# Warm-up matmuls from a constant, row tile 1 centred into its own buffer, final waits placed earlier: three small edits at the two ends of a TensorE-bound kernel

## The chip, the cores and the metric

The kernel runs on one core of a Trainium2 chip. The metric is the device time of one execution in microseconds (us). TensorE (PE in the profile) does the matmuls and PEld is its weight load; VectorE is DVE, ScalarE is ACT, GpSimd is POOL, SyncE is SP and issues all the DMA transfers. Every job also ran the kernel before on the same chip.

## The reference

```python
xn = layernorm(x)                       # x: 2048 x 512, bf16
y  = x + attention(xn) + geglu(xn)
# attention: 32 heads of 16, each query sees 8 keys at distance 0, 2, .. 14
# geglu: (gelu(xn @ w_gate) * (xn @ w_up)) @ w_down, inner size 1376
```

## The kernel before

The kernel is a graph of tasks. A list scheduler in the kernel's own code orders the tasks on each engine at build time, and another function turns dependencies into semaphore waits. So an edit at the start can change the order of matmuls far behind it.

The three places that the change touches. First, the warm-up: matmuls on a buffer of zeros that keep TensorE busy until data is there.

```python
G.task("dve", "c_wsrc", 0.25, lambda e: e.memset(wsrc[:, :], 0.0), wr=[I_wsrc], prio=PC - 1)
# ...
WARM = cfg.get("WARM", ([512] * 8 + [128], [512, 128]))   # before / behind the first transposes
for i, wn in enumerate(WARM[0] + WARM[1]):
    # ...
    e.matmul(PS[...], lhsT=wsrc[:, 0:128], rhs=wsrc[:, 0:wn], start=True, stop=True)
```

Second, row tile 1 (rows 128 to 255). Its statistics are taken on ScalarE, while VectorE does those of tile 0. ScalarE computes the sum, minus the mean, the sum of squares about the mean, the variance and the square root; VectorE subtracts the mean in place and multiplies by the reciprocal.

```python
("sxx1", 0.55, dict(out=XR[:, 0, :], func=ACTF.Square, bias=sums[:, 1:2],
                    accum_out=sums[:, 2:3]), ...),          # reads XIN row tile 1
("var1", 0.2, dict(out=mv[:, 1, 1:2], in_=sums[:, 2:3], func=ACTF.Identity, scale=1.0 / D), ...)
# ... sub1, on VectorE: in place, so it waits for sxx1
e.tensor_scalar(out=XIN[:, it.slot, t2, :], in0=XIN[:, it.slot, t2, :], scalar1=mv[:, t, 0:1],
                scalar2=None, op0=ALU.subtract)
```

ScalarE's order in the head is fixed by a chain: sum, square root 0, minus mean, squares, variance, square root 1, then the eviction of tile 0's transposes.

Third, the end. Before it ends, the kernel waits until all DMA semaphores have reached their totals. Those that don't belong to the last five DMAs are waited for just in front of the last store.

```python
if eng_name == "sp" and t is self.order["sp"][-1]:
    late = self.order["sp"][-5:]
    for (s, tot) in self.dma_totals:
        if not any(q.sem is s for q in late):
            e.wait_ge(s, tot)
```

## Time and profile before

| | before |
|---|---|
| time, median of 3 runs | 194.56 us (194.54 to 194.84) |
| span of the profiled run | 193.2 us (its own time 194.91) |
| TensorE busy | 187.6 us, 97% |
| first warm-up matmul | 1.51 us |
| first real QKV matmul | 6.23 us |
| TensorE goes on behind the second eviction | 7.95 us |
| last add ends, last store issued | 191.08, 191.26 us |

The time is a little longer than the span (194.91 against 193.20 us for the same execution). **t0** is the start of the first QKV matmul. **T** is the moment at which TensorE goes from half to full clock; it is read from the distance between starts of 128-column matmuls, 107 ns before and 56 ns after. Half and full clock are names for these two spacings: the profile's own clock column reads 1.00 on both sides of T. The **resume** is the first matmul behind ScalarE's second eviction (7.95 here): from there on TensorE is hardly ever without work. The prediction shows the lines.

### The profile page before, as it was taken

The page shows a single profiled execution, that of the slowest core. Times are in us where ns is not written, and L with a number is a line of the kernel's source. Part 1 is how long each engine was busy: PE and PEld are TensorE (multiplying, and loading weights), DVE is VectorE, ACT ScalarE, POOL GpSimd, SP SyncE. Part 2 cuts the span into 40 slices and gives each one's busy share as a digit, 9 for nine tenths or more (in the row PEclk, how much of TensorE's full clock was granted, in tenths as well). Part 3 has the DMA queues.
Part 4 walks back from the last instruction along what each step waited for, and adds up shares of the span by engine and source line. Part 5 has one row for each costly group of instructions (what it writes and reads, how often), then busy time and mean ns, then how long its engine had stood idle before and what let it go on. Part 6 is the DMA issues. An engine that isn't in the chain of part 4 may idle for free.

```text
span 193.2 us, 3285 instructions
## 1 busy us (share of the span) xinstructions
PE 187.6 (97%) x1239; PEld 92.6 (48%) x1256; DVE 152.4 (79%) x240; ACT 106.1 (55%) x177; POOL 15.7 (8%) x31
## 2 busy tenths in 40 slices
PE   6999999999999999999999999999999999999994
PEld 2794444444444444444444444444444444444484
DVE  5699999999997975999995599998996099912132
ACT  5677565786897666703376677328276720058000
POOL 6010011110931020000000000000000000000000
PEclk9999999999999999999999999999999999999999
DMA  5999997899564014975500597420250497130121
GB/s 142 352 397 327 313 171 136 215 244 226 150 128 102 3 33 132 242 144 150 151 25 27 127 243 166 117 90 0 68 132 21 112 230 163 41 112 0 48 76 44
DMA packets 34801, 27.04 MB, mean 140 GB/s; under 512 B 11265, under 2 KB 33249, under 8 KB 34785
## 3 DMA queue, kind: packets, MB, share of 16 engines
q1 hardware_dynamic: 34784, 26.83, 57.0%
q8 instruction: 10, 0.16, 0.4%
q14 instruction: 7, 0.05, 0.1%
HBM read 19.99 MB, written 5.26 MB: 131 GB/s over the span
## 4 chain that ended last, share of the span: by engine, by line
PE 97%; issue 1%; DVE 0%; DVEq 0%
PE PS L1399 36%; PE PS L1478 20%; PE PS L1156 18%; PE PS L1474 7%; PE PS L1102 4%; PE PS L1367 4%; PE PS L1240 4%; PE PS L870 2%; PE PS L1434 2%; PE PS L1233 1%; PE PS L1044 1%; DVE OB L1498 0%; DVE wsrc L819 0%; DVE Wd L843 0%; DVEq L558 0%
## 5 line engine op out<-in xcount | busy, mean ns | idle before, releaser
L1416 ACT ACTIVATE UU<-PS 128x512 bf16<-128x512 f32 x40 | 24.1, 603 | 35.7 <-PE PS L1399 35.7
L1478 PE MATMUL PS<-Wd,HT 128*128 128x512 bf16 (+2 forms) x207 | 41.1, 345 | 0.1
L1399 PE MATMUL PS<-xnT,Wu 128*128 128x512 bf16 x155 | 39.8, 379 | 0.7 <-issue 0.5
L1399 PE MATMUL PS<-xnT,Wg 128*128 128x512 bf16 x155 | 39.2, 379 | 0.5 <-ACT OT L1379 0.2
L1210 DVE TENSOR_TENSOR UNI<-QT,KT 128x2048 bf16<-128x2048 bf16 x32 | 37.0, 1219 | 2.6 <-PE PS L1367 2.5
L1156 PE MATMUL PS<-xnT,Wqkv 128*128 128x512 bf16 x156 | 35.3, 379 | 0.2
L1421 DVE TENSOR_TENSOR HT<-GG,UU 128x512 bf16<-128x512 bf16 x40 | 16.6, 419 | 20.2 <-ACT UU L1416 20.1
L1409 ACT ACTIVATE GG<-PS 128x512 bf16<-128x512 f32 x40 | 23.7, 601 | 15.0 <-PE PS L1399 12.2
L1478 PEld LDWEIGHTS PS<-Wd,HT 128*128 128x128 bf16 x209 | 19.6, 98 | 18.6
L1399 PEld LDWEIGHTS PS<-xnT,Wu 128*128 128x128 bf16 x160 | 15.3, 98 | 19.6 <-issue 1.3
L1399 PEld LDWEIGHTS PS<-xnT,Wg 128*128 128x128 bf16 x160 | 15.5, 98 | 19.3 <-ACT OT L1379 0.4
L1156 PEld LDWEIGHTS PS<-xnT,Wqkv 128*128 128x128 bf16 x160 | 15.6, 98 | 18.6
L1347 DVE TENSOR_TENSOR BS<-BS,PT 128x2048 bf16<-128x2048 bf16 x16 | 19.6, 1223 | 0.4
L1347 DVE TENSOR_TENSOR UNI<-BS,PT 128x2048 bf16<-128x2048 bf16 x16 | 19.5, 1218 | 0.0
L1498 DVE TENSOR_TENSOR OB<-PS,XR 128x512 bf16<-128x512 f32 (+2 forms) x19 | 11.2, 604 | 10.0 <-PE PS L1478 9.9
L1474 PE MATMUL PS<-Wo,OT 128*128 128x512 bf16 (+2 forms) x76 | 16.9, 345 | 0.0
L1180 ACT ACTIVATE VT<-PS 128x512 bf16<-128x512 f32 x16 | 9.6, 597 | 4.4 <-PE PS L1156 4.4
L1379 ACT ACTIVATE OT<-PS 128x512 bf16<-128x512 f32 x16 | 8.3, 602 | 5.0 <-PE PS L1367 5.0
L944 DVE BATCH_NORM_STATS2 st<-XIN 128x6 f32<-128x512 bf16 x15 | 10.1, 686 | 0.9 <-DMA XIN<-in_A_x_dram 0.9
L1474 PEld LDWEIGHTS PS<-Wo,OT 128*128 128x128 bf16 x76 | 7.2, 98 | 7.0
L1196 POOL COPY KT<-KT 128x64 bf16<-128x64 bf16 x3 | 8.0, 2657 | 17.5 <-ACT KT L1173 16.1
L1166 ACT ACTIVATE QT<-PS 128x512 bf16<-128x512 f32 x12 | 7.2, 597 | 3.1 <-PE PS L1156 3.1
(73 smaller groups left out, 153.6 us busy)
## 6 DMA issues: line engine op xcount, KB each, us to landing
BS<-vt_scratch SPq DMA_DIRECT2D x64, 128.5 KB, 3.7
vt_scratch<-VT SPq DMA_DIRECT2D x16, 128.0 KB
XR<-in_A_x_dram SPq DMA_DIRECT2D x16, 128.0 KB, 2.3
out_dram<-OB SPq DMA_DIRECT2D x14, 128.0 KB, 1.8
Wqkv<-in_A_wqkv_dram SPq DMA_DIRECT2D x3, 512.0 KB
XIN<-in_A_x_dram SPq DMA_DIRECT2D x6, 256.0 KB, 4.5
Wg<-in_B_w_gate_dram SPq DMA_DIRECT2D x1, 1280.0 KB
Wu<-in_B_w_up_dram SPq DMA_DIRECT2D x1, 1280.0 KB
```

Source lines behind the costliest of these rows:

```text
L944: return lambda e: e.bn_stats(out=st[:, t, :], in_=XIN[:, it.slot, t2, :])
L1156: ins = e.matmul(PS[:, 512 * it.slot:512 * it.slot + HWD], lhsT=lhsT, rhs=xnT[:, itx.slot, kt, c0:c0 + HWD], start=(kt == 0), stop=(kt == 3))
L1180: return lambda e: e.activation(out=VT[:, ito.slot, 0:HWD], in_=PS[:, 512 * it.slot:512 * it.slot + HWD], func=ACTF.Identity)
L1210: return lambda e: e.tensor_tensor(out=UNI[:, it.slot, :, :], in0=bass.AP(QT, (itq.slot * 4 + g) * 512, [[NQT * 4 * 512, 128], [0, 4], [1, ...
L1347: return lambda e: e.tensor_tensor(out=dst(), in0=bass.AP(BS, it.slot * 4 * 514 + o, [[NBS * 4 * 514, 128], [514, 4], [128, 4], [1, 128]]) ...
L1399: ins = e.matmul(PS[0:M, 512 * it.slot:512 * it.slot + 512], lhsT=Wx[:, kt, j * 128:j * 128 + M], rhs=xnT[:, itx.slot, kt, :], start=(kt = ...
L1409: return lambda e: e.activation(out=GG[0:M, ito.slot, :], in_=PS[0:M, 512 * it.slot:512 * it.slot + 512], func=ACTF.Gelu_apprx_tanh)
L1416: return lambda e: e.activation(out=UU[0:M, ito.slot, :], in_=PS[0:M, 512 * it.slot:512 * it.slot + 512], func=ACTF.Identity)
L1421: return lambda e: e.tensor_tensor(out=HT[0:M, ito.slot, j, :], in0=GG[0:M, ig.slot, :], in1=UU[0:M, iu.slot, :], op=ALU.mult)
L1474: ins = e.matmul(PS[:, 512 * it.slot:512 * it.slot + CW], lhsT=OT[:, ito.slot, dq, ti * 128:(ti + 1) * 128], rhs=Wo[:, dq, c0:c1], start=( ...
L1478: ins = e.matmul(PS[:, 512 * it.slot:512 * it.slot + CW], lhsT=HT[:, ith.slot, j, ti * 128:(ti + 1) * 128], rhs=Wd[:, j, c0:c1], start=Fal ...
L1498: return lambda e: e.tensor_tensor(out=OB[:, ito.slot, 0:CW], in0=PS[:, 512 * it.slot:512 * it.slot + CW], in1=XR[:, itx.slot, c0:c1], op= ...
```

## The change

The intent: let TensorE's warm-up start at once instead of behind a memset, take two links out of the chain that normalizes row tile 1, and let the last store go out as soon as its data is there. The diff, cut to its core:

```diff
-            if eng_name == "sp" and t is self.order["sp"][-1]:
-                late = self.order["sp"][-5:]
+            if eng_name == "sp" and t is self.order["sp"][-4]:
+                late = self.order["sp"][-7:]
 ...
-            for q in self.order["sp"][-5:]:
+            for q in self.order["sp"][-7:]:
 ...
-        wsrc = sb("wsrc", [128, 512], BF)
+        one_l = nc.const_aps.tensor(1.0, [128, 128], BF)
+        one_r = nc.const_aps.tensor(1.0, [128, 512], BF)
+        XS = sb("XS", [128, 512], BF)
 ...
-        G.task("dve", "c_wsrc", 0.25, lambda e: e.memset(wsrc[:, :], 0.0), wr=[I_wsrc], prio=PC - 1)
-        WARM = cfg.get("WARM", ([512] * 8 + [128], [512, 128]))
+        WARM = cfg.get("WARM", ([512] * 9 + [128], [512, 128, 128, 128, 128]))
 ...
-                            ("var1", 0.2, dict(out=mv[:, 1, 1:2], in_=sums[:, 2:3], func=ACTF.Identity,
-                                               scale=1.0 / D), [(I_sums, 2)], [(I_mv, "v1")])):
+                    if t == 1:
+                        return lambda e: e.activation(out=sq[:, 1:2], in_=sums[:, 2:3], func=ACTF.Sqrt,
+                                                      scale=1.0 / D, bias=eps[:, 0:1])
 ...
+                        return lambda e: e.tensor_scalar(
+                            out=XS[:, :], in0=XIN[:, it.slot, 1, :], scalar1=mv[:, 1, 0:1], scalar2=None,
+                            op0=ALU.subtract)
 ...    # the multiplication for tile 1 then reads XS and writes XIN
```

More of the change, by code (lines that the diff above doesn't have):

```diff
@@ L674, in bass_parallel_sum__sliding_local_dilated__glu_gated_geglu__prompt_kernel @@
     NXIN = cfg.get("NXIN", 4)
-    NSUBA = cfg.get("NSUBA", 0)
     NSQA = cfg.get("NSQA", 4)
@@ L800, in bass_parallel_sum__sliding_local_dilated__glu_gated_geglu__prompt_kernel @@
         I_zpad = Item("zpad")
-        I_wsrc = Item("wsrc")
         I_onef = Item("onef")
@@ L809, in bass_parallel_sum__sliding_local_dilated__glu_gated_geglu__prompt_kernel @@
         I_sums = Item("sums")
+        I_xs = Item("XS")
         I_junk = Item("junk")
@@ L869, in mk_w @@
             def mk_w(it=it_warm, wn=wn):
-                return lambda e: e.matmul(PS[:, 512 * it.slot:512 * it.slot + wn], lhsT=wsrc[:, 0:128],
-                                          rhs=wsrc[:, 0:wn], start=True, stop=True)
-            t_w = G.task("pe", "warm%d" % i, d_mm(wn), mk_w(), rd=[I_wsrc], wr=[it_warm], prio=-400, mode="f")
+                return lambda e: e.matmul(PS[:, 512 * it.slot:512 * it.slot + wn], lhsT=one_l,
+                                          rhs=one_r[:, 0:wn], start=True, stop=True)
+            t_w = G.task("pe", "warm%d" % i, d_mm(wn), mk_w(), wr=[it_warm], prio=-400, mode="f")
             t_w.urgent = True
@@ L951, in bass_parallel_sum__sliding_local_dilated__glu_gated_geglu__prompt_kernel @@
                             ("sxx1", 0.55, dict(out=XR[:, 0, :], func=ACTF.Square, bias=sums[:, 1:2],
-                                                accum_out=sums[:, 2:3]), [(I_sums, 1)], [I_junk, (I_sums, 2)]),
-                            ("var1", 0.2, dict(out=mv[:, 1, 1:2], in_=sums[:, 2:3], func=ACTF.Identity,
-                                               scale=1.0 / D), [(I_sums, 2)], [(I_mv, "v1")])):
+                                                accum_out=sums[:, 2:3]), [(I_sums, 1)], [I_junk, (I_sums, 2)])):
                         def mk_a(kw=kw, it=it_x):
@@ L978, in bass_parallel_sum__sliding_local_dilated__glu_gated_geglu__prompt_kernel @@
                 if t < NSQA:
-                    t_of["sq%d" % t] = G.task("act", "sq%d" % t, 0.15, mk_sa(), rd=[(I_mv, "v1" if t == 1 else t), I_eps],
+                    t_of["sq%d" % t] = G.task("act", "sq%d" % t, 0.15, mk_sa(), rd=[(I_sums, 2) if t == 1 else (I_mv, t), I_eps],
                                               wr=[(I_sq, t)], prio=pr - 100, table="sqrt")
@@ L1003, in mk_sub @@
                         scalar2=None, op0=ALU.subtract)
-                if t < NSUBA:
-                    def mk_sub(t=t, t2=t2, it=it_x):
-                        return lambda e: e.activation(
-                            out=XIN[:, it.slot, t2, :], in_=XIN[:, it.slot, t2, :], func=ACTF.Identity,
-                            scale=-1.0, bias=mv[:, t, 0:1])
-                t_of["sub%d" % t] = G.task("act" if t < NSUBA else "dve", "sub%d" % t,
-                                           0.6 if t < NSUBA else 0.27, mk_sub(), rd=[(it_x, t2), (I_mv, t)],
-                                           wr=[(it_x, t2)], prio=tp0(t) + 2)
+                if t == 1:
+                    def mk_sub(it=it_x):
+                        return lambda e: e.tensor_scalar(
+                            out=XS[:, :], in0=XIN[:, it.slot, 1, :], scalar1=mv[:, 1, 0:1], scalar2=None,
+                            op0=ALU.subtract)
+                t_of["sub%d" % t] = G.task("dve", "sub%d" % t, 0.27, mk_sub(), rd=[(it_x, t2), (I_mv, t)],
+                                           wr=[I_xs if t == 1 else (it_x, t2)], prio=tp0(t) + 2)
                 def mk_nm(t=t, t2=t2, it=it_x):
-                    if t < NSUBA:
-                        return lambda e: e.tensor_scalar(
-                            out=XIN[:, it.slot, t2, :], in0=XIN[:, it.slot, t2, :], scalar1=rstd[:, t:t + 1],
-                            scalar2=-1.0, op0=ALU.mult, op1=ALU.mult)
                     return lambda e: e.tensor_scalar(
-                        out=XIN[:, it.slot, t2, :], in0=XIN[:, it.slot, t2, :], scalar1=rstd[:, t:t + 1],
+                        out=XIN[:, it.slot, t2, :], in0=XS[:, :] if t == 1 else XIN[:, it.slot, t2, :], scalar1=rstd[:, t:t + 1],
                         scalar2=None, op0=ALU.mult)
-                t_of["norm%d" % t] = G.task("dve", "norm%d" % t, 0.27, mk_nm(), rd=[(it_x, t2), (I_rstd, t)],
+                t_of["norm%d" % t] = G.task("dve", "norm%d" % t, 0.27, mk_nm(), rd=[I_xs if t == 1 else (it_x, t2), (I_rstd, t)],
                                             wr=[(it_x, t2)], prio=tp0(t) + 4)
@@ L1134, in bass_parallel_sum__sliding_local_dilated__glu_gated_geglu__prompt_kernel @@
                                wr=[(it_qt, ("t", t)) if which == 0 else (KTI[0], ("t", t))], prio=-100 + t)
-                chain(["sx1", "sq0", "negm1", "sxx1", "var1", "sq1", "evx0_0", "evx0_1", "evq0_0", "sq2"])
+                chain(["sx1", "sq0", "negm1", "sxx1", "sq1", "evx0_0", "evx0_1", "evq0_0", "sq2"])
                 chain(["evx1_0", "sq3"])
```

## The prediction

A gain of 0.24 us for the head was my estimate. The sum came to 0.24 (head) + 0.16 (final waits) + 0 (middle) = 0.40 us, and so to 194.15.

> **What bounds the kernel now.** I read the page first, then the timeline of the first 14 us, then the windows, then the timeline of the last 10 us with the SyncE queue by itself. The page (engine totals, then the 40 slices):
>
> ```profile
> PE 187.6 (97%) x1239; PEld 92.6 (48%) x1256; DVE 152.4 (79%) x240; ACT 106.1 (55%) x177; POOL 15.7 (8%) x31
> ...
> PE   6999999999999999999999999999999999999994
> ```
>
> TensorE (PE) has work in every slice but the first and the last. The windows say the same: in 15.0 to 190.8 us it is busy for 174.20 of 175.80 us. What stays the same amount of matmul work can only be shifted as a whole: time is to be had before TensorE is saturated (the head) and after its last matmul (190.8 to 193.2, the tail). The span of the profiled run is 193.2 us against 194.91 us of its time; I carry a shift of the span over to the time one for one.
>
> The head, in the timeline:
>
> ```profile
> 1.18 0.27 DVE L819 MEMSET wsrc<- 128x256 uint32 x1
> ...
> 1.51 3.70 PE L870 MATMUL PS<-wsrc 128*128 128x512 bf16 x9 [1.51 <-DVE wsrc L819]
> ...
> 4.63 0.35 DVE L1018 TENSOR_SCALAR XIN<-XIN,rstd 128x512 bf16<-128x512 bf16 x1
> ...
> 5.04 0.61 PE L1044 MATMUL PS<-ident,XIN 128*128 128x128 bf16 x4
> ...
> 5.37 0.21 ACT L956 ACTIVATE mv<-sums 128x1 bf16<-128x1 f32 x1
> 5.37 0.35 DVE L1001 TENSOR_SCALAR XIN<-XIN,mv 128x512 bf16<-128x512 bf16 x1 [0.32 <-ACT XR L956]
> 5.44 0.74 PE L870 MATMUL PS<-wsrc 128*128 128x512 bf16 x2
> 5.61 0.30 ACT L976 ACTIVATE sq<-mv,eps 128x1 bf16<-128x1 bf16 x1
> ...
> 5.81 0.36 ACT L1064 ACTIVATE xnT<-PS 128x256 bf16<-128x256 bf16 x1
> 5.94 0.16 DVE L994 RECIPROCAL rstd<-sq 128x1 f32<-128x1 bf16 x1
> 6.14 0.35 DVE L1018 TENSOR_SCALAR XIN<-XIN,rstd 128x512 bf16<-128x512 bf16 x1
> 6.23 1.02 PE L1102 MATMUL PS<-xnT,Wqkv 128*128 128x128 bf16 x8
> ...
> 7.51 0.39 ACT L1064 ACTIVATE xnT<-PS 128x256 bf16<-128x256 bf16 x1 [1.34 <-PE PS L1044]
> ```
>
> The columns are start, duration, engine, line, operation, output from input, count, and in brackets the idle time and what ended it. The warm-up waits for the memset of its source and starts at 1.51. Row tile 0 is normalized at 4.98 (4.63 + 0.35), transposed from 5.04 to 5.65, evicted by ScalarE by 6.17, and the first real QKV matmuls start at 6.23. Row tile 1 is normalized at 6.49, its transposes stand behind those eight matmuls, its eviction ends at 7.90, and TensorE goes on at 7.95. From there to 14.8 it never waits long, so 7.95 is the time to beat.
>
> The windows on TensorE (length, busy time, count):
>
> ```profile
> 6.22:7.05 0.83, 0.82 (x8) 1.00 1.13 338
> ...
> 7.95:9.74 1.79, 1.78 (x32) 1.00 1.14 339
> ```
>
> The same 128-column matmul costs 0.83 / 8 = 104 ns at 6.2 and 1.79 / 32 = 56 ns at 8. Single records put the switch at 7.08: starts 107 ns apart until then, 56 ns after. The clock column says 1.00 throughout, so it doesn't show this; the spacing does.
>
> The tail, in the timeline and in SyncE's queue alone:
>
> ```profile
> 190.26 0.33 SPq L1505 DMA_DIRECT2D out_dram<-OB  x1
> 190.78 0.29 DVE L1498 TENSOR_TENSOR OB<-PS,XR 128x128 bf16<-128x128 f32 x1 [0.55 <-PE PS L1478]
> 191.26 0.33 SPq L1505 DMA_DIRECT2D out_dram<-OB  x1
> ```
>
> The last add is done at 191.08, but its store is issued at 191.26. The store before was issued 0.03 us after its add (ended 190.24, issued 190.26). Between them SyncE works through ten semaphore instructions from 190.65 to 191.22 (61 ns apart, for 19 semaphores), begun when the issue of the store before was over.
>
> [...] I expect the same 427 ns per 512-column matmul as now; no run shows it yet. [...] the last store here takes 1.47 us from the start of its issue (191.26) to the end of the wait for it (192.73), and nothing in the change touches that.
>
> **The change part by part.**
>
> Warm-up source. The memset (0.27) and the wait for it go. TensorE passes the start barrier at 0.78; ScalarE's and VectorE's first work begins at 0.79 and 0.91, so I take 0.90 for the first warm-up matmul, 0.6 earlier. There are nine instead of eight of 512 columns and one of 128: 9 x 0.427 + 0.107 = 3.95 us at half clock, ending at 4.85, before row tile 0 is ready (4.98). So they delay nothing. The transposes still start at 5.04: that chain hangs on the first x tile (VectorE begins its statistics at 2.91, on a DMA). After the transposes come 512 + 4 x 128 columns instead of 512 + 128: at half clock 0.427 + 4 x 0.107 = 0.85, ending at 5.44 + 0.85 = 6.30; at full clock 0.21 + 4 x 0.056 = 0.44, ending by 5.7. What the earlier start is worth is thus decided by when the clock switches.
>
> Row tile 1. The subtraction now writes a buffer of its own, so it no longer waits for ScalarE's sum of squares: it can run when the mean is there, at 5.08 instead of 5.37. The 0.21 us ScalarE step for the variance goes, and the square root takes the sum with a scale: it runs at 5.37 to 5.67 instead of 5.61 to 5.91. ScalarE then takes the eviction of tile 0 at once: with transposes at half clock (data at 5.65) at about 5.69, so 6.05 and first QKV at 6.11; at full clock (data at about 5.45) at 5.57, so 5.93 and first QKV at 5.99. The last packet of the Q weights lands at 5.91 in the trace's landing events, so these would just be there. The normalization of tile 1 ends at 6.27 at full clock (6.49 before), early enough not to hold its transposes.
>
> Two ends for the head. Clock up before 5.04: first eight matmuls 5.99 to 6.44, transposes of tile 1 to 6.66, their data at 6.83, eviction (0.39) to 7.25, TensorE goes on at 7.31: 0.64 earlier than the 7.95 of this profile, but only 0.24 earlier than the old kernel with an equally early switch (there 6.23 + 0.45 + 0.22 + 0.17 + 0.03 + 0.39 + 0.06 = 7.55). Clock up only at 7.08 or so: the longer filler holds the first QKV matmuls to 6.30, and the head is 0.07 later than before. [...] between, the head ends proportionally from its best to its worst. [...] Gain: 0.24. That the old times lie 0.30 apart (194.54 to 194.84) fits a head that varies by 0.4.
>
> Final waits. They go in front of the fourth last store, issued at 187.92, where SyncE is idle for 1.26 us (186.66 to 187.92); 17 semaphores in nine instructions at 61 ns are 0.55 us, which is hidden. The last store follows its add by 0.03: 191.26 becomes 191.10, gain 0.16. Behind it stand seven instead of five semaphores; the instruction listing pairs them so that the last store's wait is still followed by only one more. Zero.
>
> Middle. The list scheduler moves work in the saturated part: two feed-forward groups more before the first attention reduction, two more before the first probability-value reduction, one less between the second logit reduction and the first output accumulation. The last leaves 2.17 + 0.16 + 0.86 = 3.2 us between that reduction and the accumulation, where ScalarE needs 2.07 + about 0.2 for its four evictions: covered. Idle of TensorE there is only 1.6 us in all[...], so little can be won; I count 0 +- 0.3.
>
> Sum: 0.24 + 0.16 + 0 = 0.40; 194.56 - 0.40 = 194.16, say 194.15.
>
> **The rivals.** (1) The clock switches early almost always[...]. Then 194.9 profiled would drop by 0.8, and the time to 193.8. [...] (2) The clock comes late as before, the filler of 0.85 us becomes the wait in place of the one removed, and only the tail stays: 194.4 to 194.5. For it: the switch at 7.08 in this profile; against: an earlier start can hardly make it later. (3) The reordering exposes a wait in the middle, for instance the output accumulation on ScalarE's evictions: up to +0.5, 194.7. For it: the tuned priorities were left as they were; against: the slack above. (4) An x or weight load binds the shorter head: the K weights land at 7.77, needed from about 8.2 at the earliest; the gate weights land at 15.91, needed at 16.8. Not bound.
>
> **Range and chances.** Rivals 1 and 3 with margin give 193.65 to 194.75. A change of 2% is 3.9 us, more than head and tail together could give or a moved wait is likely to cost: 0.01 faster, 0.98 within, 0.01 slower.
>
> **What would show it.** First warm-up matmul near 0.9; transposes of tile 0 still near 5.0; ScalarE's eviction of tile 0 about 0.1 to 0.25 earlier; the spacing of 128-column matmuls changing from 107 to 56 ns before 7.0; TensorE resuming after the second eviction between 7.3 and 8.0; last store 0.03 after its add. I am wrong if the constant operand slows the warm-up, if the last store still waits, or if TensorE idles over 2 us between 15 and 190.

## The result, and the profile after

| | before | after |
|---|---|---|
| time, median | 194.57 us (194.54 to 194.84, 4 runs) | 194.28 us (194.23 to 194.35, 4 runs) |
| span of the profiled run | 193.2 us | 192.5 us |
| warm-up starts | 1.51 | 0.83 |
| T | 7.06 to 7.15 | 6.02 to 6.11 |
| t0 | 6.23 | 6.17 |
| resume | 7.95 | 7.47 |
| last add ends, last store issued | 191.08, 191.26 | 190.59, 190.62 |

The ratio is 0.9982 with a 95% interval of 0.9965 to 1.0: the same at 2%, 0.29 us less by the medians. A ratio is the mean time of one kernel's runs over that of the other's of the same rounds, so not quite the ratio of the medians.

The page of the kernel after, the engine totals and the slices of TensorE:

```profile
PE 187.8 (98%) x1244; PEld 92.8 (48%) x1260; DVE 151.7 (79%) x239; ACT 105.9 (55%) x176; POOL 15.6 (8%) x31
...
PE   8999999999999999999999999999999999999995
```

Only the first and the last slice differ, the first by two tenths (6 to 8), the last by one (4 to 5). The head in its timeline (start, duration, engine, line, operation, output from input, count, idle time before and what ended it):

```profile
0.83 4.11 PE L870 MATMUL PS<-const-bfloat16-1.0 128*128 128x512 bf16 x10 [0.83 <-PEq L1548]
...
4.57 0.35 DVE L1014 TENSOR_SCALAR XIN<-XIN,rstd 128x512 bf16<-128x512 bf16 x1
...
4.98 0.61 PE L1040 MATMUL PS<-ident,XIN 128*128 128x128 bf16 x4
5.02 0.35 DVE L1007 TENSOR_SCALAR XS<-XIN,mv 128x512 bf16<-128x512 bf16 x1
...
5.31 0.30 ACT L975 ACTIVATE sq<-sums,eps 128x1 bf16<-128x1 f32 x1
5.38 0.95 PE L870 MATMUL PS<-const-bfloat16-1.0 128*128 128x512 bf16 x5
5.63 0.38 ACT L1060 ACTIVATE xnT<-PS 128x256 bf16<-128x256 bf16 x1
...
6.17 0.61 PE L1098 MATMUL PS<-xnT,Wqkv 128*128 128x128 bf16 x8
...
7.04 0.38 ACT L1060 ACTIVATE xnT<-PS 128x256 bf16<-128x256 bf16 x1 [1.03 <-PE PS L1040]
```

The subtraction (5.02) no longer has the 0.32 us of waiting for ScalarE in its bracket, the square root stands at 5.31 instead of 5.61, and the eviction at 5.63 instead of 5.81. The first eight QKV matmuls take 0.61 instead of 1.02 us to the end of the last one: they run at full clock. The tail:

```profile
190.30 0.29 DVE L1494 TENSOR_TENSOR OB<-PS,XR 128x128 bf16<-128x128 f32 x1 [0.55 <-PE PS L1474]
```
```profile
190.62 0.33 SPq L1501 DMA_DIRECT2D out_dram<-OB  x1
```

The store follows its add (190.30 + 0.29 = 190.59) by 0.03 us.

Where did the time go? In the two profiled runs the resume moved by 7.955 - 7.474 = 0.48 us, and the last add moved by 191.075 - 190.594 = 0.48 us. Not one hundredth was won or lost between the two, although the scheduler had reordered the feed-forward matmuls there. The store then went out 0.16 us sooner. So the spans differ by 193.20 - 192.55 = 0.65 us, and that is head plus tail, to 0.01. But the medians of the times differ by 0.29 only. The profile of before must have caught an execution with a late head. Its own time, 194.91, is above all the other runs of that first set. What makes a head late or early is the question for the experiments.

### The profile page after: what moved, and what is told of

Its sections match the earlier page's. It is cut to its first block, busy times and chain, and to the rows that moved or that the text cites. A ratio compares the mean times of both kernels' runs of the same rounds, so it can differ in the third digit from the quotient of the medians.

```text
span 192.5 us, 3287 instructions
## 1 busy us (share of the span) xinstructions
PE 187.8 (98%) x1244; PEld 92.8 (48%) x1260; DVE 151.7 (79%) x239; ACT 105.9 (55%) x176; POOL 15.6 (8%) x31
## 4 chain that ended last, share of the span: by engine, by line
PE 95%; issue 1%; DMA 1%; DVE 0%; ACT 0%; SPq 0%; DVEq 0%
PE PS L1395 36%; PE PS L1474 20%; PE PS L1152 18%; PE PS L1470 7%; PE PS L1363 4%; PE PS L1098 4%; PE PS L1236 4%; PE PS L1430 2%; DMA XIN<-in_A_x_dram 1%; PE PS L1229 1%; PE PS L1040 1%; PE PS L870 0%; SPq L927 0%; DVE XIN L1014 0%; DVE OB L1494 0%
```

## The experiments

My theory: T is different in each execution, whatever the kernel (an assumption of the prediction); the warm-up part moves T by the 0.68 us by which TensorE starts sooner (1.51 to 0.83), the row tile 1 part moves t0, the final waits move the last store, and the middle is worth nothing. Rivals: one part carries all of it; the gain is constant and the spread is noise; the reordered middle costs or gives. The texts on record count spans to the last recorded instruction, 0.05 us before the span's end; the table below counts to the end, so 185.19 and 185.02 there are 185.24 and 185.07 here.

All profiles, in one table. The last column is the span minus the resume, so everything behind the head:

| run | warm-up starts | T between | t0 | resume | span | rest |
|---|---|---|---|---|---|---|
| before | 1.51 | 7.06 and 7.15 | 6.23 | 7.95 | 193.20 | 185.25 |
| e5 (before again) | 1.51 | 4.90 and 5.03 | 6.22 | 7.54 | 193.10 | 185.56 |
| e1 (tail only) | 1.51 | 6.80 and 6.87 | 6.19 | 7.78 | 192.85 | 185.07 |
| e2 (warm-up only) | 0.83 | 6.39 and 6.49 | 6.28 | 7.69 | 192.93 | 185.24 |
| e2b (the same) | 0.83 | 6.09 and 6.17 | 6.24 | 7.56 | 192.80 | 185.24 |
| e3 (tile 1 only) | 1.51 | 7.37 and 7.46 | 6.12 | 8.05 | 193.29 | 185.24 |
| e3b (the same) | 1.51 | 5.86 and 6.43 | 6.43 | 7.74 | 193.15 | 185.41 |
| after | 0.83 | 6.02 and 6.11 | 6.17 | 7.47 | 192.55 | 185.07 |
| e6 (after again) | 0.83 | 4.63 and 4.96 | 5.92 | 7.23 | 192.31 | 185.08 |
| e6b (after again) | 0.83 | 6.63 and 6.72 | 6.32 | 7.80 | 192.88 | 185.07 |
| e4 (short filler) | 0.84 | 5.76 and 6.23 | 6.23 | 7.53 | 192.61 | 185.07 |
| e8 (Q load split) | 0.83 | 5.32 and 5.40 | 6.04 | 7.36 | 193.02 | 185.67 |
| e7 (no warm-up) | 5.00 | 8.92 and 9.00 | 6.30 | 8.38 | 194.01 | 185.63 |

### e1: the final waits alone

```diff
-            if eng_name == "sp" and t is self.order["sp"][-1]:
-                late = self.order["sp"][-5:]
+            if eng_name == "sp" and t is self.order["sp"][-4]:
+                late = self.order["sp"][-7:]
 ...
-            for q in self.order["sp"][-5:]:
+            for q in self.order["sp"][-7:]:
```

> The kernel before with only the final waits moved; TensorE's order is unchanged. My theory: the last store is issued 0.03 us after its add instead of 0.19, the semaphore waits fit into SyncE's idle time, and the time falls by 0.16 us (0.10 to 0.20). Rival (the waits only move, or the transfer of the last store is bounded by the store ahead of it): the landing of the last store does not move and the time is within 0.05 of before. Head unchanged: first QKV matmul at about 6.2.

Measured: 194.68 us median (194.41 to 195.43, 6 runs) against 194.62 (194.49 to 196.62, 11 runs); ratio 0.9993, interval 0.9959 to 1.0026. The expected 0.16 us does not show in the times: the runs of one kernel lie a whole microsecond apart. The profile does show it. VectorE's and SyncE's last work in the timeline of e1:

```profile
190.61 0.29 DVE L1498 TENSOR_TENSOR OB<-PS,XR 128x128 bf16<-128x128 f32 x1 [0.55 <-PE PS L1478]
```
```profile
190.93 0.33 SPq L1505 DMA_DIRECT2D out_dram<-OB  x1
```

Add done at 190.90, store at 190.93, and the rest is 185.07 instead of 185.25. So in a profile this part is worth 0.17 to 0.18 us, and the times alone could not have told.

### e2 and e2b: the warm-up alone

```diff
-        wsrc = sb("wsrc", [128, 512], BF)
+        one_l = nc.const_aps.tensor(1.0, [128, 128], BF)
+        one_r = nc.const_aps.tensor(1.0, [128, 512], BF)
 ...    # memset and its item taken out, operands exchanged
-        WARM = cfg.get("WARM", ([512] * 8 + [128], [512, 128]))
+        WARM = cfg.get("WARM", ([512] * 9 + [128], [512, 128, 128, 128, 128]))
```

> The kernel before with only the warm-up part (constant operand, 9 and 5 matmuls); TensorE's order is that of the changed kernel. My theory: the warm-up starts at 0.83, the first QKV matmuls still wait for ScalarE's eviction at about 6.17 to 6.23 (or for the filler until 6.30 if the clock is late), and the gain is only what an earlier clock switch brings: 0.0 to 0.2 us in the time, with the 128-column spacing changing to 56 ns before 7.0. Rival A (the warm-up part is the whole head gain): the same head as the changed kernel, TensorE resuming after the second eviction at 7.47. Rival B (the reordered middle costs): slower than before.

Measured: 194.73 us median (194.50 to 194.83, 6 runs), ratio 0.9988 (0.9957 to 1.0019). The resume was at 7.69, not 7.47. But T was later too (6.4 instead of 6.1), and the longer filler, which ended at 6.28, held t0 to 6.28; whether this part is the whole head gain is better read from e2b, whose T was that of the changed kernel. TensorE's order was that of the changed kernel and the rest 185.24, as before: the reordered middle costs nothing, which rejects rival B.

> The kernel before with the warm-up part alone, once more, for a second switch time and more times. From the runs so far: with t0 the start of the first QKV matmul and T the switch to full clock, TensorE resumes after the second eviction at t0 + 1.31 if T is before t0, and 0.48 us later for each us by which T is after t0 (up to t0 + 1.3); the span is that plus 185.19 (old final waits). Theory: this part alone moves T by -0.68 us in the mean and leaves t0 at 6.2 to 6.3 whatever T is, as ScalarE's variance and square root still stand before the eviction; resume at 7.5 to 7.85, times 194.45 to 194.85, no run at 195 or above. Rival (the warm-up part also moves t0): t0 at 6.1 or below.

Measured: 194.52 us median (194.49 to 194.93, 5 runs), ratio 0.9996 (0.9984 to 1.0009). In its timeline ScalarE's eviction and the QKV matmuls stand where they stood before, although the clock rose at 6.1, and the resume was 7.56, not 7.47. So this part is not the whole head gain:

```profile
5.82 0.36 ACT L1063 ACTIVATE xnT<-PS 128x256 bf16<-128x256 bf16 x1
...
6.24 0.62 PE L1101 MATMUL PS<-xnT,Wqkv 128*128 128x128 bf16 x8
```

Over both, 11 runs: none above 194.93. Of the 37 runs of the kernel before over all jobs (the five of e5 not counted), ten were above that (up to 195.41, and one of 196.62). This fits a part that cuts off the late heads and leaves the early ones as they were: its lowest, 194.49, is not below the 194.41 of before. It is not shown, though: if the two kernels' times were spread alike, all ten would still fall among the 37 in about one case of twenty (my estimate from these counts).

### e3 and e3b: row tile 1 alone

```diff
# from the changed kernel: old final waits and old warm-up; its source in an unused slot, as memory is full
+        G.task("dve", "c_wsrc", 0.25, lambda e: e.memset(OB[:, 3, :], 0.0), wr=[I_wsrc], prio=PC - 1)
-                return lambda e: e.matmul(..., lhsT=one_l, rhs=one_r[:, 0:wn], ...)
+                return lambda e: e.matmul(..., lhsT=OB[:, 3, 0:128], rhs=OB[:, 3, 0:wn], ...)
-        WARM = cfg.get("WARM", ([512] * 9 + [128], [512, 128, 128, 128, 128]))
+        WARM = cfg.get("WARM", ([512] * 8 + [128], [512, 128]))
```

> The changed kernel with the warm-up (old counts, memset source; the source lies in a slot of the output buffer that is unused until much later, as there is no room for both buffers) and the final waits undone, so only the row tile 1 part is left; TensorE's order is that of before. My theory: square root for tile 1 at about 5.3, eviction of tile 0 ends by about 6.05, first QKV matmul at about 6.10 instead of 6.23, so 0.10 to 0.15 us gained whatever the clock does; if the clock switches at 7.0 the eight matmuls stay at 107 ns. Rival (this chain is not the one that holds TensorE): within 0.05 of before.

Measured: 194.78 us median (194.37 to 195.10, 6 runs), ratio 0.9988 (0.9953 to 1.0024). t0 came at 6.12, as expected, 0.11 sooner than before. The clock was later than in any other profile with a warm-up (7.4). Here a sooner t0 is worth only half: by the relation told under e7, the kernel before with T at 7.41 would resume at 8.11, and this one resumed at 8.05. So 0.06, not 0.10 to 0.15: what is started sooner runs at half clock until T (107 ns a matmul instead of 56), so only half as much is done in the time gained. I had not thought of that.

> The row tile 1 part alone, once more. Theory: it leaves T where it is in the kernel before [...] and moves t0: to 6.05 to 6.12 when T is after 5.6, and to 5.9 to 6.0 when T is before the transposes at 5.0; resume by the same relation, span that plus 185.19; times from 194.2 up to 195.2, as spread as those of the kernel before but lower by 0.05 (late T) to 0.25 (early T). Rival (the part does not move t0, or the spread shrinks): t0 at 6.2 or times within 0.3 us of each other.

Measured: 194.75 us median (194.21 to 194.87, 6 runs), ratio 0.9995 (0.9981 to 1.0009). The times spread as expected, and 194.21 is lower than any of the 37 runs of before. But t0 was 6.43, which I had not expected:

```profile
6.43 0.61 PE L1098 MATMUL PS<-xnT,Wqkv 128*128 128x128 bf16 x8 [0.26 <-DVE XIN L1014]
```

The bracket names VectorE, which had long been done with what TensorE needs. TensorE's wait names the Q weights' semaphore, passed at 6.32, and the trace's landing events put their last packet at 6.30. In the other profiles they landed between 5.54 and 6.16. The times of e3 and e3b decide nothing, as their intervals reach over 1; e3's profile shows what the part does, and e3b's what else can hold t0.

### e4: the short filler

```diff
-        WARM = cfg.get("WARM", ([512] * 9 + [128], [512, 128, 128, 128, 128]))
+        WARM = cfg.get("WARM", ([512] * 9 + [128], [512, 128]))
```

> The changed kernel with the filler behind the first transposes as before, 512 + 128 instead of 512 + 4 x 128 columns. In the changed kernel's profile the first QKV matmul starts at 6.17, just as the filler ends, while ScalarE's eviction was done at 6.01. My theory: the filler is what binds, so the QKV matmuls start at about 6.08 and the time falls by a further 0.05 to 0.10 us against the changed kernel (about 194.20). Rival (the filler [...] brings the clock switch forward; or the Q weights' landing binds): the clock switches later or the start stays at 6.15, and the time is equal or above that of the changed kernel.

Measured: 194.36 us median (194.29 to 194.56, 6 runs), ratio 0.9973 (0.9942 to 1.0004); nothing that tells it from the changed kernel. In this run the Q weights landed at 6.09 and t0 was 6.23, so my theory failed here: with the filler gone, the Q weights bound. The filler binds in e6b: there the clock was late, the filler ended at 6.31 and t0 was 6.32, against 6.30 in the prediction. In this one profile the switch to full clock came no later than in the others without the three short matmuls.

### e5 and e6, e6b: the same kernels again

> The kernel before, unchanged, for a second profile of it. Phase theory: another T than 7.09, t0 at 6.2 to 6.25 even when T is early, resume by the relation, span that plus 185.19; ratio to the kernel before 1.000 within 0.002. Rival (the profile of before was typical of the kernel and T is fixed): T at 7.09 and resume 7.95 again.

Measured: 194.82 us median (194.53 to 195.07, 5 runs), ratio 1.0007 (0.9994 to 1.002). TensorE in its timeline:

```profile
5.03 0.40 PE L1044 MATMUL PS<-ident,XIN 128*128 128x128 bf16 x4
...
6.22 0.62 PE L1102 MATMUL PS<-xnT,Wqkv 128*128 128x128 bf16 x8 [0.52 <-ACT xnT L1064]
```

The clock was up before the transposes at 5.03 (0.40 us instead of 0.61), two microseconds sooner than in the first profile of the very same kernel. And still t0 was 6.22: TensorE then idles 0.52 us for ScalarE. The resume was 7.54, against 7.55 in the prediction for an early switch in the old kernel. One thing was not as expected: the rest was 185.56 instead of 185.24. The last add and the last store:

```profile
190.37 0.29 DVE L1498 TENSOR_TENSOR OB<-PS,XR 128x128 bf16<-128x128 f32 x1 [0.55 <-PE PS L1478]
```
```profile
191.18 0.33 SPq L1505 DMA_DIRECT2D out_dram<-OB  x1
```

Here 0.52 us lie between the end of the add (190.66) and the store. The issues of the two stores ahead took 0.86 and 0.42 us instead of 0.33, so SyncE came to its ten wait instructions later, at 190.56, and they still took their 0.6 us. The same is seen in e3b (an issue of 0.51 us, 0.37 us to the store). With the new waits a slow issue costs the last store nothing as long as SyncE is free again before the last add ends: in e8 two took 0.68 and 0.42 us, and the last store was still 0.03 us behind its add. In e7 one took 0.97 us, past the end of the last add, and it was 0.21 us.

> The changed kernel unchanged, for more times and a second profile. Theory (phase): the instant at which the matmul spacing goes from 107 to 56 ns lies anywhere [...]from run to run and sets when TensorE resumes after the second eviction; from there to the end the span is 185.02 us whatever the head did. So this profile has another switch time than 6.06, its resume plus 185.02 is the span within 0.02, and the times spread, from 194.2 up to about 194.8, wider than the 194.23 to 194.35 of the first four runs; the kernel before spreads from 194.5 to above 195.3. Rival (the gain is a fixed amount and the spread is noise of the chip): switch at 6.06 again, times within 0.15 of each other.

Measured: 194.41 us median (194.02 to 195.04, 6 runs) against 194.82 (194.47 to 195.31, 11 runs); ratio 0.9984 (0.9968 to 1.0). TensorE in its timeline:

```profile
4.96 0.40 PE L1040 MATMUL PS<-ident,XIN 128*128 128x128 bf16 x4
5.20 0.61 PE L870 MATMUL PS<-const-bfloat16-1.0 128*128 128x512 bf16 x5
5.92 0.61 PE L1098 MATMUL PS<-xnT,Wqkv 128*128 128x128 bf16 x8
```

This is the counterpart of e5: the clock was up before the transposes, and now t0 is 5.92 and the resume 7.23, 0.31 sooner than e5 with an equally early clock. That is the row tile 1 part at its best: e6 has the other two parts as well, but what e5 waited for was ScalarE's eviction, and that ended at 5.85 here instead of 6.17. The spread of a microsecond says that the narrow range of the first four runs was luck.

> The changed kernel once more, as e6_after_again: a third switch time and six more times. Phase theory: resume plus 185.02 us is the span again, and over both repeats the upper end of the times falls by about 0.3 us or more against the upper end of the kernel before in the same rounds, as the switch comes up to 0.68 us earlier in the late cases. Rival: the two kernels' times differ by a constant only.

Measured: 194.58 us median (194.27 to 194.73, 5 runs), ratio 0.9982 (0.9968 to 0.9997). A third T (6.7) and the same rest, 185.07. The upper ends: 195.04 over both repeats against 195.31 of before in the same rounds, 0.27 lower, a little short of the 0.3 expected.

### e7: no warm-up

```diff
-        WARM = cfg.get("WARM", ([512] * 9 + [128], [512, 128, 128, 128, 128]))
+        WARM = cfg.get("WARM", ([], []))
```

> The changed kernel without any warm-up matmul. Theory: TensorE's first work is the transposes at about 5.0, so the switch to 56 ns can come only [...] and the QKV matmuls until then cost double: about half of the time between 7 and the switch, 0.5 to 2.5 us more than the changed kernel, 195 to 197 us, with the largest spread of all kernels. Rival (the warm-up gives little, since the real work of the head waits for other engines anyway): within 0.3 us of the changed kernel.

Measured: 196.70 us median (195.72 to 197.67, 4 runs), ratio 1.0093 (1.0063 to 1.0124); one run lies above the 197 expected. The expected 0.5 to 2.5 us were my estimate. T was 8.9 to 9.0, 3.9 us after the first transpose, and the QKV matmuls ran at 107 ns until then. The rest of 185.63 holds 0.3 us of that (T is behind the resume) and the slow issue told above. The warm-up as such is worth about 2 us (194.41 and 194.58 with it, in e6 and e6b); the change only moved it.

From these profiles a relation can be put together, which I used for the expectations of the last three runs. Behind t0 come twelve matmuls (8 for QKV, 4 transposes), 0.67 us at full clock, then 0.64 us until ScalarE's second eviction is there: the resume is t0 + 1.31. Each microsecond by which T lies after t0 adds 1 - 56/107 = 0.48 us, up to the 1.28 us that the twelve take at half clock. It gives 7.23 for e6 (measured 7.23), 7.53 for e5 (7.54), 7.54 for e4 (7.53), 7.74 for e3b (7.74), 7.96 for before (7.95), 8.04 for e3 (8.05).

### e8: a try at a faster version

```diff
-        WARM = cfg.get("WARM", ([512] * 9 + [128], [512, 128, 128, 128, 128]))
+        WARM = cfg.get("WARM", ([512] * 9 + [128], [512, 128]))
 ...    # the load of the Q weights: columns 0 to 255 first, then
+        G.task("sp", "ld_wq1", 0, lambda e: e.dma_start(
+            Wqkv[:, :, 256:512], A_wqkv[:, 256:512].rearrange("(k p) n -> p k n", p=128)),
+            wr=[(I_wq, "q1")], prio=-957.9, nbytes=256 * 1024)
```

> An attempt at a faster version: the changed kernel with the short filler (512 + 128) and the load of the Q weights in two halves, of which the first QKV matmuls need only the first. In the short-filler run they waited for the Q weights until 6.12, 0.15 us after ScalarE's eviction. Theory: the first QKV matmuls start at about 6.05, bound by ScalarE's eviction, and with an early clock switch the resume comes at 7.35 to 7.4; in late-switch runs nothing is gained. Median 0.0 to 0.1 us below the changed kernel, 194.2 to 194.3. Rival: the additional transfer delays the x tiles and K weights behind it, and the K weights (needed at about 8.2) become the wait, so that it is 0.1 to 0.4 us slower.

Measured: 194.87 us median (194.66 to 195.50, 6 runs), ratio 1.0004 (0.9989 to 1.002): worse than the changed kernel. The first half of my theory held (t0 6.04, resume 7.36 with an early clock), and so did the rival. TensorE in its timeline:

```profile
8.84 0.84 PE L1102 MATMUL PS<-xnT,Wqkv 128*128 128x128 bf16 x12 [0.42 <-DMA Wqkv<-in_A_wqkv_dram]
```

The K weights, queued behind one more transfer, landed at 8.80 instead of 7.65 to 8.2, and the rest grew from 185.07 to 185.67. Between the starts of the last matmul ahead of this wait and the first behind it lie 0.64 us instead of 0.06, and these 0.58 are nearly all of the growth of the rest (0.60). I found no version that beats the changed kernel.

## Why the prediction was right

The time, 194.28, lies in the range and 0.13 from the predicted 194.15. That it lies so near is in part luck: over the 15 runs of all jobs the changed kernel's mean is 194.44, and that of the kernel before 194.76 (one run of 196.62 left out), not 194.56. Step by step:

**Warm-up.** It started at 0.83 (I took 0.90), the constant operand ran at 427 ns per 512 columns, and the transposes still began at 4.98: as predicted. The part's worth is what an earlier T brings, and T did differ from run to run: 3.4 to 5.9 us after TensorE's first matmul over all thirteen profiles. That a start 0.68 earlier moves T by 0.68 in the mean, as my theory had it, is not shown: T has the mean 6.5 in the five profiles begun at 1.51 and 5.9 in the seven begun at 0.83, but it scatters by 1.0 and 0.6, so the difference of 0.6 is uncertain by 0.5. One step of the working was wrong: between an early and a late clock the head was to go "proportionally from its best to its worst". With the old row tile 1 it stays at its best until T passes t0: the resume was 7.54 with T at 5.0 (e5) and 7.56 with T at 6.1 (e2b).

**Row tile 1.** Subtraction 5.02 (5.08), square root 5.31 (5.37), eviction 5.63 to 6.01 at half clock (5.69 to 6.05), t0 with an early clock 5.92 (5.99), resume 7.23 (7.31). The prediction gave this part to the head as a whole; e5 against e6, both with an early clock, shows t0 moved by 0.30 us (6.22 to 5.92), and e2b, without this part, still has 6.24.

**Filler.** The prediction's "the longer filler holds the first QKV matmuls to 6.30" came out as 6.32 in e6b and 6.28 in e2.

**Final waits.** 0.16 predicted; 0.16 to 0.18 in the profiles without a slow issue. What I had not seen is that the old place also passes on a slow issue just ahead of it (e3b, e5); one of 0.46 us two stores ahead, in e2b, cost nothing. The last store itself took as long as before: 1.46 us from the start of its issue to the end of the wait for it (190.62 to 192.08), against 1.47.

**Middle.** Zero predicted, zero measured to 0.02 us: e2, with the new order of matmuls, has the same rest as e3, with the old one.

**The sum.** If a term is mis-sized, it is the head, put at 0.24 by the estimate. The medians of the first rounds give 0.29 in all, so 0.12 for it. Over all jobs, with the one run of 196.62 left out, the mean of 36 runs of before is 194.76 and that of 15 runs of after 194.44: 0.32 in all, 0.15 for the head. The runs of either kernel scatter by 0.26 (standard deviation), which puts about 0.08 on that difference, so it is not clearly apart from 0.24. Even the 0.15 may hold some of the tail: slow issues made the rest 0.17 and 0.32 longer in two of the six profiles with the old waits (e3b, e5), and 0.28 in one of the seven with the new (e7). One reason for less is shown: the Q weights' landing varied from 5.54 to 6.30 while I took the one value of 5.91, and in e3b, e4 and e7 it held t0. How much that takes in the mean isn't measured.

**The rivals.** Rival 1 (the clock switches early almost always) fell: of the seven profiles that began at 0.83, six switched after 5.3. Rival 2 (the filler takes the place of the wait removed) is true of some executions, e6b for one. Rival 3 (a wait in the middle) fell. Rival 4 was too quickly put aside: the K weights had enough room in the kernel as it is, the Q weights had not.

Open: what made one run of before 196.62; there is no trace of it. Open too: why a store's issue on SyncE is sometimes slow. The last four stores took 0.33 us each as a rule, but one or two of them took 0.42 to 0.97 in five of the thirteen profiles (e2b, e3b, e5, e7, e8).

## What to carry to other kernels

Where one engine is saturated, cut the time into head, middle and tail and compare them one by one: here the middle was the same to 0.02 us, and a change of 0.17 us that the times could not show stood plainly in the tail of the profile. Before two profiles are set against each other, look for what differs between executions of the same kernel: these two differed by 0.65 us, while the means of all runs differ by 0.32, so half of it was the luck of one execution's clock. Do waits that only collect what is long done while the queue is idle, not in front of the last transfer (here worth 0.16 to 0.18 us).
